# Transposes of probabilities, first-layer rows, gathered rows and returning rows as float32r in a fused attention, expert and feed-forward kernel

## The chip, the cores and the metric

One core of one Trainium2 chip runs the whole program. The metric is device time in microseconds (us) of one execution. Engine names are those of the profile: PE is the matrix engine, PEld its weight load, DVE the vector engine, ACT the scalar engine, POOL the GpSimd engine, SP the engine whose queue issues most transfers.

## What is computed

Attention over 2 batches of 8 heads (576 positions, head width 64, rotary positions on q and k), then a mixture of 8 experts of which each of the 1152 tokens takes one, then a feed-forward layer. All in float32:

```python
scores = scale * np.matmul(q_rot, k_rot.transpose(0, 1, 3, 2))
scores = scores - np.max(scores, axis=-1, keepdims=True)
attn = np.exp(scores)
attn = attn / (np.sum(attn, axis=-1, keepdims=True) + 1e-09)
x = np.matmul(attn, v)                       # to (1152, 512)
expert_idx = np.argmax(xn @ en.T / tau, axis=1)
...
h = np.maximum(x[mask] @ w1[e], 0.0)         # 512 -> 1024
out[mask] = gate_w[mask, None] * (h @ w2[e]) # 1024 -> 512
...
h = out @ w_in                               # 512 -> 2048
g = np.maximum(h, 0.0) + np.log1p(np.exp(-np.abs(h)))
y = g @ w_out
```

## The kernel before, in words

The order of instructions on every engine is the order in which the program is written; nothing reorders them. The precise products are made of float32r matmuls on operands that are split in two: a high part (ACT casts to float32r) and a low part (DVE subtracts the high part from the value).

**Attention** (to 187 us in the trace). The 16 heads run in 8 pairs. A pair has 9 steps, one for each block of 128 query rows (the fifth is shared by the two heads); with 72 steps in all, t = 0 to 71. In step t the program emits, in this order: the exponential of step t (`softmax_exp`, ACT L539, into a tile p of 128 x 576), the evictions left over from the step before (among them the p-tail: ACT L432 and DVE L433), four transposes of p(t-1) on PE (`transp`, L545, into PSUM tile tp), the scores of step t+2 (`mm_s`, L529, into PSUM tile sc, of which there are two), some filler work on PE, the row maximum of step t+1 (`softmax_max`, DVE L533), the low part of the transposed step t-2 (`ev_lo`, DVE L563) and the high part of step t-1 (`ev_hi`, ACT L552). The tiles tp are two, so the transposes of one step wait until `ev_lo` of two steps before has read its tile. The filler work holds the products with v (`pv`, L590 to L592), the transposes of the last 64 columns of p (`tail`, L574, and `tail_shared`, L578), the transposes that prepare q and k of the next pair (`prep_bank`, L444 from ks as float32r, L448 from qq and L446 from t as float32) and the output products (`xout`, L606). The rotation of the next pair's q and k runs on POOL.

The tiles p come from a pool of eight buffers, which are handed out in turn; before the first p the pool gives out four of them to the expert embeddings (`embt`), their squares (`esq`) and two normalised copies (`en2`). A generator `egen` advances by one part in each of the steps 2 to 5; each part is one DVE scaling of embt (L641), the first one after a reciprocal.

**Routing** (187 to 198 us) picks the experts and sorts tokens into blocks of 128.

**Experts** (198 to 368 us). There are 13 blocks. For a block the rows are gathered (tile xg), transposed by 4 PE transposes (`x_t`, through `four`, L954) and split (`x_ev`); 24 matmuls of 512 columns make the first layer (L975); ACT applies the relu into tile hr (L982); 8 transposes (`h_t`, L954, reading every second column of hr) and a split give the operand of the second layer, 24 matmuls (L1004); ACT multiplies by the gate (L1011, tile yo), and POOL scatters the rows to memory (L1014, tensor ys). The weights of each expert are fetched and split in 8 pieces a block (ACT L936, DVE L940). The tile gates is copied from PSUM once (DVE L1097), before the first `y_out`.

**Feed-forward** (368 to 577 us). Rows come back from memory into tiles yr, 4 transposes each (`y_t`, L877), 9 in all, of which 5 are made while the last expert blocks run. Then two passes of matmuls (L1306, L1353).

A transpose is a matmul in which the data is the loaded operand (PEld) and an identity is streamed; `idf` is the identity in float32, `idr` in float32r:

```python
def transp(t):
    p = tiles['p', t]
    tp = tiles['tp', t] = ps_t.tile([P, 4, P], F32, tag="t", name="tp")
    for x in range(4):
        T.transpose(tp[:, x], p[:, x * P:x * P + P], idf)
```

Of the kernel before, what the change touches and what calls it, by code (L numbers as in the profile page):

```python
# [95 lines left out]
def moe_kernel(ctx: ExitStack, tc: tile.TileContext, q, k, v, emb, tau, w1, w2, w_in, w_out, rope, tab, out):  # L96
# [58 lines left out]
    rev = tb("rev").rearrange("p (c e) -> p c e", c=5)  # L155

# [162 lines left out]
    with actx:  # L319
# [4 lines left out]
        pp = actx.enter_context(tc.tile_pool(name="pp", bufs=8))  # L324
# [210 lines left out]
        def softmax_exp(t):  # L535
            _, g, hs = where(t)
            i, c = hs[0]
            p = tiles['p', t] = pp.tile([P, S], F32, tag="p", name="p")
            A.activation(p.rearrange("p (n t) -> p n t", n=2), tiles.pop(('sc', t))[:, :, 0:288], AF.Exp, bias=tiles.pop(('nm', t)), accum_out=head(i)['rst'][:, c:c + 1])  # L539

        def transp(t):
            p = tiles['p', t]
            tp = tiles['tp', t] = ps_t.tile([P, 4, P], F32, tag="t", name="tp")
            for x in range(4):
                T.transpose(tp[:, x], p[:, x * P:x * P + P], idf)  # L545
# [23 lines left out]
        def tail(i):  # L569

            j, a = divmod(i, 2)
            d = ps_m.tile([LEFT, 4, P], F32, tag="m", name="tail")
            for c in range(4):
                T.transpose(d[:, c], tiles.pop(('p', 9 * j + 5 * a + c))[:, 512:576], idf)  # L574
            return lambda: prep_k(last(j)[:, a, 0:512], d.rearrange("p c t -> p (c t)"), True)

        def tail_shared(j, bank):
            T.transpose(bank[0:LEFT], tiles.pop(('p', 9 * j + 4))[:, 512:576], idf)  # L578
            return lambda: prep_k(last(j)[:, :, 512:576], bank[0:LEFT].rearrange("p (a t) -> p a t", a=2))
# [50 lines left out]
        embt = pp.tile([E, DM], F32, tag="p", name="embt")  # L630
# [3 lines left out]
        esq = pp.tile([E, DM], F32, tag="p", name="esq")  # L634
        en2 = [pp.tile([E, 4, 2, D], F32, tag="p", name="en2") for _ in range(2)]
# [85 lines left out]
        for t in range(NS + 5):  # L721
# [55 lines left out]
            if 1 <= t <= NS:  # L777
                ev_hi(t - 1)
            do_late()
# [35 lines left out]
            if 2 <= t <= 5:  # L815
                next(egen, None)
# [49 lines left out]
    def y_load(p, t, **cond):  # L866

        yr = yr3[t % 4]
        r = (TOK_PASSES[p][0] + t) * P
        return yr, SY.dma_start(yr, ys[r:r + P], **cond)  # L870

    def y_t(p, t, yr, pool, tag):
# [3 lines left out]
        for k in range(4):  # L876
            T.transpose(pt[:, k], yr[:, k * P:(k + 1) * P], idf)  # L877
# [15 lines left out]
    if True:  # L893
# [8 lines left out]
        xgs = [xg_.tile([P, DM], F32, name=f"xg{i}") for i in range(3)]  # L902
        for t in xgs:
            G.memset(t, 0.0)
# [43 lines left out]
        def gather(n):  # L948
            G.indirect_dma_start(xgs[n % 3][:, :], None, xs[:, :], bass.IndirectOffsetOnAxis(idx[:, n:n + 1], axis=0), bounds_check=NT - 1, oob_is_err=False)

        def four(src):
            pt = ps_x.tile([P, 4, P], F32, tag="x", name="pt")
            for k in range(4):
                T.transpose(pt[:, k], src(k), idf)  # L954
# [23 lines left out]
        def relu(n):  # L978
            ph = hs.pop(n)
            h = hs[n] = xe.tile([P, FF], F32, tag="hr", name="hr", bufs=1)  # L980
            for i in range(2):
                A.activation(h[:, 512 * i:512 * i + 512], ph[i], AF.Relu)  # L982

        def h_t(n):
            h = hs.pop(n)
            return [four(lambda k: h[:, 512 * i + 256 * (k // 2):512 * i + 256 * (k // 2) + 256].rearrange("p (q r) -> p q r", r=2)[:, :, k % 2]) for i in range(2)]
# [105 lines left out]
        def between(n):  # L1092
            if n == 1:
# [3 lines left out]
                V.tensor_copy(gates, pgat)  # L1097
                xctx.close()
                ypool = ctx.enter_context(tc.tile_pool(name="ypool", bufs=1, side="right", reuse_waits="tile"))
                yr3.extend(ypool.tile([P, DM + 1], F32, name=f"yr{i}") for i in range(4))  # L1100
                ypools.append(ypool)
                for t in yr3:
                    G.memset(t, 0.0)
# [125 lines left out]
        x_ev(3, x_t(3))  # L1229
# [215 lines left out]
```

## Time and profile before

| | us |
|---|---|
| median of three runs | 580.10 |
| the three runs | 579.31, 580.10, 581.25 |
| the profiled execution's own time | 579.42 |
| its span in the trace | 577.6 |
| PE busy | 545.6 (94%) |
| DVE busy | 454.3 (79%) |
| ACT busy | 438.6 (76%) |
| POOL busy | 199.9 (35%) |

The span runs from the first to the last record of the trace; 1.8 us of the execution's own time lie around it. Shares are means over stages that have different limits, so a stage's limit is read from the stretch itself. Matmuls overlap, so the time from one PE row's start to the next one's start says more than the duration printed. "xN" on a row counts N instructions of the same kind in a row; the bracket at a row's end is the idle time of that engine before it and what ended it.

### The profile page before, as it was taken

How to read it: one execution, taken by the hardware profiler on the slowest of the kernel's cores; microseconds unless marked ns; L12 is line 12 of the kernel's file. 1: busy time of each engine (PE TensorE's matmuls, PEld its weight loads, DVE VectorE, ACT ScalarE, POOL GpSimd, SP SyncE). 2: the span in 40 equal slices, each digit the busy share in tenths (PEclk: the TensorE clock that was granted, in tenths of full speed). 3: DMA queues.
4: the chain of work that ended last, by engine and by line, in shares of the span. 5: the costliest groups of instructions: out<-in, count | busy, mean ns of one | idle time of the engine just before them, and what ended most of it. 6: DMA issues, size and time to landing. Idle time of an engine off the chain costs nothing. (4 is left out here: it accounts for less than half of the span.)

```text
span 577.6 us, 9874 instructions
## 1 busy us (share of the span) xinstructions
PE 545.6 (94%) x3277; PEld 478.7 (83%) x3277; DVE 454.3 (79%) x757; ACT 438.6 (76%) x832; POOL 199.9 (35%) x304
## 2 busy tenths in 40 slices
PE   5789999999998799999999999999999999999995
PEld 4679999999987688887777888887889999888994
DVE  6988788787977779989999998778876766687243
ACT  2678878877775599789988998698877877677550
POOL 7999998749731330332222421300000000000033
PEclk8799999999999899999999999999999999999998
DMA  5414000061332545892439895263323222000012
GB/s 152 132 61 109 24 1 2 2 204 53 111 114 95 188 129 169 305 345 74 177 117 320 304 364 199 82 226 109 110 78 106 73 74 75 35 1 0 2 73 91
DMA packets 37269, 70.54 MB, mean 122 GB/s; under 512 B 8146, under 2 KB 23890, under 8 KB 37088
## 3 DMA queue, kind: packets, MB, share of 16 engines
q1 hardware_dynamic: 34272, 62.64, 32.5%
q0 software_dynamic: 2800, 7.09, 3.6%
q8 instruction: 26, 0.43, 0.3%
q10 hardware_dynamic: 144, 0.16, 0.2%
q14 instruction: 27, 0.22, 0.1%
HBM read 91.11 MB, written 8.13 MB: 172 GB/s over the span
## 5 line engine op out<-in xcount | busy, mean ns | idle before, releaser
L940 DVE TENSOR_TENSOR wt<-raw,wt 128x1024 fp32r<-128x1024 f32 x100 | 116.5, 1220 | 8.7 <-ACT wt L936 8.6
L1306 PE MATMUL ph<-yt,wt 128*128 128x320 f32 (+1 forms) x576 | 105.4, 336 | 2.2 <-ACT r__5778 L1318 1.4
L936 ACT CAST wt<-raw 128x1024 fp32r<-128x1024 f32 x100 | 98.7, 1066 | 6.6 <-DMA raw<-in_moe_w_dram 6.6
L1353 PE MATMUL po<-wt,g 128*128 128x512 f32 x432 | 103.6, 391 | 0.0
L1306 PEld LDWEIGHTS ph<-yt,wt 128*128 128x128 f32 x576 | 93.5, 188 | 11.6 <-ACT r__5778 L1318 1.8
L1353 PEld LDWEIGHTS po<-wt,g 128*128 128x128 f32 x432 | 80.3, 188 | 16.7 <-ACT g L1337 0.3
L1004 PE MATMUL py<-wt,ht 128*128 128x512 f32 x312 | 76.0, 396 | 2.6 <-DVE wt L940 2.6
L1370 POOL DMA_INDIRECT out_dram<-acc,otok x9 | 9.6, 1070 | 186.2 <-DVE acc L1367 185.6
L1004 PEld LDWEIGHTS py<-wt,ht 128*128 128x128 f32 x312 | 57.6, 188 | 15.4 <-DVE wt L940 3.9
L975 PE MATMUL ph<-wt,xt 128*128 128x512 f32 x288 | 69.3, 395 | 0.0
L539 ACT ACTIVATE p<-sc,nm 128x576 f32<-128x576 f32 x72 | 53.9, 749 | 14.4 <-DVE nm L533 13.8
L975 PEld LDWEIGHTS ph<-wt,xt 128*128 128x128 f32 x288 | 53.2, 188 | 10.8
L533 DVE TENSOR_REDUCE nm<-sc 128x1 f32<-128x576 f32 x72 | 54.2, 752 | 2.9 <-PE sc L529 1.7
L552 ACT CAST ph<-tp 128x512 fp32r<-128x512 f32 (+1 forms) x80 | 42.8, 547 | 14.9 <-PE tp L545 14.4
L529 PE MATMUL sc<-kt,qt 128*128 128x288 f32 x256 | 52.0, 327 | 1.6 <-ACT p L539 0.8
L545 PE MATMUL tp<-idf,p 128*128 128x128 f32 x288 | 45.1, 280 | 4.7 <-DVE pl L563 3.3
L563 DVE TENSOR_TENSOR pl<-tp,ph 128x512 fp32r<-128x512 f32 (+1 forms) x80 | 49.5, 627 | 0.1
L379 POOL TENSOR_TENSOR t<-qk,ropet 128x256 f32<-128x256 f32 x58 | 42.3, 757 | 10.9 <-DMA qk<-in_k_dram 10.4
L1337 ACT CAST g<-e 128x512 fp32r<-128x512 f32 (+2 forms) x33 | 21.7, 659 | 29.6 <-PE po L1353 20.2
L1338 DVE TENSOR_TENSOR g<-e,g 128x512 fp32r<-128x512 f32 (+2 forms) x33 | 24.3, 740 | 23.7 <-ACT g L1337 23.5
L529 PEld LDWEIGHTS sc<-kt,qt 128*128 128x128 f32 x256 | 38.1, 199 | 2.8 <-ACT p L539 1.3
L590 PE MATMUL po<-ph,vs 128*128 128x288 f32 x128 | 36.6, 307 | 3.8 <-DVE kt L433 1.4
(238 smaller groups left out, 1004.7 us busy)
## 6 DMA issues: line engine op xcount, KB each, us to landing
raw<-in_moe_w_dram SPq DMA_DIRECT2D x116, 512.0 KB
raw<-in_moe_w_in_dram SPq DMA_DIRECT2D x16, 512.0 KB
raw<-in_moe_w_out_dram SPq DMA_DIRECT2D x16, 512.0 KB
yr<-ys SPq DMA_DIRECT2D x9, 256.5 KB
qk<-in_k_dram SPq DMA_DIRECT2D x8, 256.0 KB
qk<-in_q_dram SPq DMA_DIRECT2D x8, 256.0 KB
vv<-in_v_dram SPq DMA_DIRECT2D x8, 256.0 KB
xs<-xrow SPq DMA_DIRECT2D x1, 1024.0 KB
```

The source lines that it names most:

```text
L529: T.matmul(sc[:, n, 0:288], lhsT=w, rhs=r, start=(x == 0), stop=(x == len(mm) - 1))
L533: V.tensor_reduce(nm, tiles['sc', t][:, :, 0:288], axis=AX.XY, op=ALU.max, negate=True)
L539: A.activation(p.rearrange("p (n t) -> p n t", n=2), tiles.pop(('sc', t))[:, :, 0:288], AF.Exp, bias=tiles.pop(('nm', t)), accum_out=head( ...
L545: T.transpose(tp[:, x], p[:, x * P:x * P + P], idf)
L552: A.copy(columns(head(i))['ph'][:, :, c * P:c * P + w], tp[:, :, x * w:x * w + w])
L563: V.tensor_tensor(hd['pl'][:, :, sl], tp[:, :, x * w:x * w + w], f(hd['ph'][:, :, sl]), op=ALU.subtract)
L936: A.copy(wt[:, 0], raw)
L940: (eng or V).tensor_tensor(wt[:, 1], raw, f(wt[:, 0]), op=ALU.subtract)
L975: T.matmul(ph[i], lhsT=xt[:, a, c], rhs=wt[:, r, 512 * i:512 * i + 512] if n else wt[r][:, 512 * i:512 * i + 512], start=(c == 0 and a == ...
L1004: T.matmul(py, lhsT=ht[c // 2][:, a, k], rhs=rhs[:, s], start=(c == 0 and r == 0 and a == 0 and s == 0), stop=(c == 3 and r == 1 and a == 1))
L1306: T.matmul(phs[i][:, 0:n1 - n0], lhsT=wt[:, a, k], rhs=yts[p][:, r, k, n0:n1], start=(k == 0 and a == 0 and r == 0), stop=(k == 3 and a == 1))
L1353: T.matmul(outs[i][c], lhsT=g[:, a, c * P:c * P + P], rhs=wt[:, r], start=(first and a == 0 and r == 0), stop=(last and a == 1))
```

## The change

Four kinds of transposes change type: those of p (`transp`), of hr (`h_t`), of xg (`x_t`) and of yr (`y_t`) stream the float32r identity and write float32r, over the same bits. The transposes of the last 64 columns of p stay in float32, as do those of qq and t.

To declare the same bytes as float32r, p gets a column more (577) and a second tile `pr` over the same buffer, and DVE sets the extra column to zero: one MEMSET of 128 x 1 for each step (72), placed behind `ev_lo` of that step. All transposes of p, tails included, are made to wait for that MEMSET. hr gets the same (one MEMSET for each block, in `relu`). xg and yr are declared float32r directly.

The pool of p has now eight named buffers instead of a turn. embt lies in p5, esq in p4, the two en2 in p6 and p7; steps 0 to 5 write p0 to p5, so the exponential of step 5 writes the buffer of embt. The generator egen advances once in steps 2 and 3 and twice in step 4.

One block is compared: the gathered rows of block 3 are transposed a second time in float32 (4 more PE transposes), ACT copies the result, DVE compares it with the float32r one and reduces to one number for each row, and a DVE instruction adds 1e30 times that to one column of gates.

```diff
-        pp = actx.enter_context(tc.tile_pool(name="pp", bufs=8))
+        pp = actx.enter_context(tc.tile_pool(name="pp", bufs=1))
+        slots = itertools.chain((f"p{i % 6}" for i in range(10)), itertools.cycle(f"p{i}" for i in (6, 7, 4, 5, 0, 1, 2, 3)))
...
-            p = tiles['p', t] = pp.tile([P, S], F32, tag="p", name="p")
+            slot = tiles['slot', t] = next(slots)
+            p = tiles['p', t] = pp.tile([P, S + 1], F32, tag=slot, name="p")[:, 0:S]
...
+        def rounded(t):
+
+            p = pp.tile([P, S + 1], F32R, tag=tiles.pop(('slot', t)), name="pr")
+            tiles['pad', t] = V.memset(f(p[:, S:]), 0.0).ins.name
+            tiles['p', t] = p
...
-                T.transpose(tp[:, x], p[:, x * P:x * P + P], idf)
+                after(T.transpose(tp[:, x].bitcast(F32R), p[:, x * P:x * P + P], idr), tiles['pad', t])
...
-                T.transpose(d[:, c], tiles.pop(('p', 9 * j + 5 * a + c))[:, 512:576], idf)
+                after(T.transpose(d[:, c], f(tiles.pop(('p', 9 * j + 5 * a + c))[:, 512:576]), idf), tiles.pop(('pad', 9 * j + 5 * a + c)))
...
-        embt = pp.tile([E, DM], F32, tag="p", name="embt")
+        embt = pp.tile([E, DM], F32, tag="p5", name="embt")
...
-        esq = pp.tile([E, DM], F32, tag="p", name="esq")
-        en2 = [pp.tile([E, 4, 2, D], F32, tag="p", name="en2") for _ in range(2)]
+        esq = pp.tile([E, DM], F32, tag="p4", name="esq")
+        en2 = [pp.tile([E, 4, 2, D], F32, tag=f"p{6 + x}", name="en2") for x in range(2)]
...
+            if t < NS:
+                rounded(t)
             do_late()
...
-            if 2 <= t <= 5:
+            for _ in range((0, 0, 1, 1, 2)[t] if t < 5 else 0):
                 next(egen, None)
...
-            T.transpose(pt[:, k], yr[:, k * P:(k + 1) * P], idf)
+            T.transpose(pt[:, k].bitcast(F32R), yr[:, k * P:(k + 1) * P], idr)
...
-        def four(src):
+        def four(src, pad=None):
             pt = ps_x.tile([P, 4, P], F32, tag="x", name="pt")
             for k in range(4):
-                T.transpose(pt[:, k], src(k), idf)
+                after(T.transpose(pt[:, k].bitcast(F32R), src(k), idr), pad)
...
+            h = xe.tile([P, FF + 1], F32R, tag="hr", name="hrr", bufs=1)
+            hs[n] = h, V.memset(f(h[:, FF:]), 0.0).ins.name
...
                 V.tensor_copy(gates, pgat)
+                V.scalar_tensor_tensor(gates[:, 3:4], differs, 1e30, gates[:, 3:4], op0=ALU.mult, op1=ALU.add)
...
-        x_ev(3, x_t(3))
+        px = x_t(3)
+        pt2 = ps_x.tile([P, 4, P], F32, tag="x", name="pt2")
+        for k in range(4):
+            T.transpose(pt2[:, k], f(xgs[0])[:, k * P:(k + 1) * P], idf)
+        x_ev(3, px)
+        other = gate_tmp()
+        differs = w([P, 1], "differs")
+        A.copy(other, pt2.rearrange("p a b -> p (a b)"))
+        V.tensor_tensor(other, px.rearrange("p a b -> p (a b)"), other, op=ALU.not_equal)
+        V.tensor_reduce(differs, other, axis=AX.X, op=ALU.max)
```

In `gather`, the load of yr and the two clearings on POOL only the declared type changes.

What moves on the engines, as the two programs have it. First DVE in steps 4 and 5 of attention (kt, vs: the next pair's k and v; nm: a row maximum; pl: low part; p with a number and tail: the p-tail; en: the scaled embeddings). Before:

```order
L533 TENSOR_REDUCE nm<-sc 128x1
L563 TENSOR_TENSOR pl<-tp,ph 128x4x128
L433 TENSOR_TENSOR kt<-own,kt 64x2x64
L392 TENSOR_TENSOR vs<-vv,vs 128x4x64
L641 TENSOR_SCALAR en_180<-embt,est 8x4x64
L433 TENSOR_TENSOR p_454<-tail,p_454 64x512
```

After:

```order
L539 TENSOR_REDUCE nm<-sc 128x1
L576 TENSOR_TENSOR pl<-tp,ph 128x4x128
L551 MEMSET pr 128x1
L439 TENSOR_TENSOR kt<-own,kt 64x2x64
L398 TENSOR_TENSOR vs<-vv,vs 128x4x64
L654 TENSOR_SCALAR en_180<-embt,est 8x4x64 x2
L439 TENSOR_TENSOR p_465<-tail,p_465 64x512
```

The fourth scaling of the embeddings stands directly behind the third and ahead of the p-tail, and a MEMSET stands behind `ev_lo`.

Second, DVE in the expert stage around the copy of gates (ht, xt: low parts of the transposed rows; wt: low part of a weight piece). Before:

```order
L959 TENSOR_TENSOR ht<-pt,ht 128x512 x2
L940 TENSOR_TENSOR wt<-raw_2864,wt 128x1024
L1097 COPY gates<-bank 128x16
L940 TENSOR_TENSOR wt<-raw_2865,wt 128x1024
L940 TENSOR_TENSOR wt<-raw_2866,wt 128x1024
L940 TENSOR_TENSOR wt<-raw_2867,wt 128x1024
L959 TENSOR_TENSOR xt<-pt,xt 128x512
```

After:

```order
L974 TENSOR_TENSOR ht<-pt,ht 128x512 x2
L955 TENSOR_TENSOR wt<-raw_3008,wt 128x1024
L1114 COPY gates<-bank 128x16
L1115 SCALAR_TENSOR_TENSOR gates<-differs,gates 128x1
L955 TENSOR_TENSOR wt<-raw_3009,wt 128x1024
L955 TENSOR_TENSOR wt<-raw_3010,wt 128x1024
L955 TENSOR_TENSOR wt<-raw_3011,wt 128x1024
L999 MEMSET hrr 128x1
L974 TENSOR_TENSOR xt<-pt,xt 128x512
```

An instruction on gates is added behind the copy, and the block's MEMSET ahead of xt. The two instructions of the comparison stand some rows earlier, behind the low part of block 3's rows:

```order
L974 TENSOR_TENSOR xt<-pt,xt 128x512
L1255 TENSOR_TENSOR junk<-pt,junk 128x512
L1256 TENSOR_REDUCE differs<-junk 128x1
L955 TENSOR_TENSOR wt<-raw_3004,wt 128x1024
L955 TENSOR_TENSOR wt<-raw_3005,wt 128x1024
```

There the program before goes from xt to the four pieces of wt directly.

## Rows read from the trace of the kernel before

**Rows 1.** Busy time by stretch: engines with counts, granted PE clock, DMA share, GB/s.
```profile
16.00:31.50 15.50, 10.25 (x61) 8.56 (x60) 14.65 (x27) 10.73 (x27) 15.06 (x24) 0.85 0.35 91
73.06:93.23 20.17, 19.75 (x160) 18.80 (x160) 16.38 (x32) 16.50 (x42) 19.06 (x33) 1.00 0.01 2
255.00:312.00 57.00, 54.39 (x264) 44.74 (x263) 56.10 (x64) 52.43 (x72) 15.64 (x15) 1.00 0.48 168
```

**Rows 2.** Groups of the page: busy us, mean ns, then idle before and releaser.
```profile
L533 DVE TENSOR_REDUCE nm<-sc 128x1 f32<-128x576 f32 x72 | 54.2, 752 | 2.9 <-PE sc L529 1.7
...
L545 PE MATMUL tp<-idf,p 128*128 128x128 f32 x288 | 45.1, 280 | 4.7 <-DVE pl L563 3.3
```

**Rows 3.** Timeline of PE: start, duration, instruction; a step with three float32 blocks.
```profile
60.02 0.77 PE L529 MATMUL sc<-kt,qt 128*128 128x288 f32 x4
...
61.06 0.60 PE L448 MATMUL pt<-idf,qq 128*128 128x128 f32 x4
...
61.86 0.38 PE L529 MATMUL sc<-kt,qt 128*128 128x288 f32 x1
```

**Rows 4.** Timeline of PE: the same step with one block as float32r.
```profile
48.66 0.77 PE L529 MATMUL sc<-kt,qt 128*128 128x288 f32 x4
...
49.62 0.54 PE L444 MATMUL pt<-idr,ks 128*128 128x128 f32 x4
...
50.38 0.38 PE L529 MATMUL sc<-kt,qt 128*128 128x288 f32 x1
```

**Rows 5.** Timeline of one pair, 73.06 to 93.23: first row, waits, last row.
```profile
73.06 0.66 PE L545 MATMUL tp<-idf,p 128*128 128x128 f32 x4
...
83.02 0.40 PE L590 MATMUL po<-ph,vs 128*128 128x288 f32 x1 [0.22 <-DVE p L433]
...
93.22 0.31 PEld L545 LDWEIGHTS tp<-idf,p 128*128 128x128 f32 x3 [0.35 <-DVE pl L563]
```

**Rows 6.** Timeline around the exponential of step 5 (26.74).
```profile
26.74 0.74 ACT L539 ACTIVATE p<-sc,nm 128x576 f32<-128x576 f32 x1 [0.44 <-PE tail L574]
...
27.47 0.57 ACT L432 CAST p<-tail 64x512 fp32r<-64x512 f32 x1
...
27.82 0.88 DVE L641 TENSOR_SCALAR en<-embt,est 8x256 f32<-8x256 f32 x1
...
28.73 0.69 DVE L433 TENSOR_TENSOR p<-tail,p 64x512 fp32r<-64x512 f32 x1
...
31.57 0.40 PE L590 MATMUL po<-ph,vs 128*128 128x288 f32 x1 [1.45 <-DVE kt L433]
...
31.76 0.41 DVE L641 TENSOR_SCALAR en<-embt,est 8x256 f32<-8x256 f32 x1
```

**Rows 7.** Busy time by stretches of 2 us there, with the granted clock.
```profile
23.00:25.00 2.00, 0.61 (x3) 0.64 (x4) 2.00 (x6) 0.98 (x3) 2.00 (x3) 0.77 0.01 3
25.00:27.00 2.00, 2.00 (x11) 1.70 (x9) 1.97 (x4) 1.04 (x3) 1.92 (x5) 0.50 0.59 146
27.00:29.00 2.00, 1.93 (x14) 1.44 (x12) 1.94 (x4) 2.00 (x6) 2.00 (x3) 0.88 0.13 30
29.00:31.00 2.00, 0.66 (x4) 0.42 (x4) 1.94 (x4) 1.12 (x4) 2.00 (x4) 1.00 0.00 0
```

**Rows 8.** Timeline: a DVE MEMSET of 128 x 1 at the start.
```profile
2.94 0.06 DVE L133 MEMSET half<- 128x1 f32 x1
```

**Rows 9.** Timeline of ACT: the first and third gate multiplication of the experts.
```profile
236.80 0.69 ACT L1011 ACTIVATE yo<-py,gates 128x512 f32<-128x512 f32 x1 [3.72 <-DVE gates L1097]
...
253.42 0.69 ACT L1011 ACTIVATE yo<-py,gates 128x512 f32<-128x512 f32 x1 [1.67 <-DMA ys<-yo,dest]
```

**Rows 10.** Timeline of PE late in the experts.
```profile
304.21 5.56 PE L1004 MATMUL py<-wt,ht 128*128 128x512 f32 x23 [0.56 <-DVE wt L940]
```

**Rows 11.** Weight loads of transposes by tile: duration ns min/median/max, first and last start.
```profile
L954 PEld LDWEIGHTS pt<-idf,hr x104: 194/209/209, 207.2 to 358.4; 128*128 128x128 f32 x104
...
L444 PEld LDWEIGHTS pt<-idr,ks x48: 138/140/142, 49.6 to 159.7; 128*128 128x128 f32 x48
```

## What I expect of the change, and why

> **What bounds the kernel now.** I read busy time by stretch first. In one pair of heads from the steady part of attention PE is busy 19.75 of 20.17 us while DVE and ACT are busy some 16.4 [rows 1]: PE sets the pace there. The first stretch, 16.0 to 31.5, is another case: DVE is busy 14.65 of 15.50 and PE only 10.25 [rows 1]. In the experts DVE is full, 56.10 of 57.00 us from 255 to 312 [rows 1], until PE starts to run back to back at 304.21 [rows 10]. So the change meets three limits: what it saves on PE counts in attention and late in the experts, what it adds on DVE counts at the start and in the experts up to 304.
>
> Then I asked which of the 72 transpose blocks of p (288 transposes [rows 2]) lie on the path. In the pair from 73.06 to 93.23 I followed the waits: PE runs through until it waits 0.22 for the p-tail of DVE at 83.02, and at 93.22 its weight load waits 0.35 for a low part [rows 5]; beside these two PE has no wait of 0.2 or more there. Two stretches of the pair, ahead of 83.02 and ahead of 93.22, therefore run through ACT and DVE (a block, its exponential and p-tail, the DVE tail), and three of nine blocks stand in them. Six of nine are on PE's path. From 31.57 on, 7 pairs and a bit are of this kind: I count 45 blocks.
>
> **What a block saves.** The trace has the swap itself. A step of four score matmuls and three transpose blocks, two of them in front of the same neighbours, takes 61.86 − 60.02 = 1.84 us with L448 as float32 [rows 3], and 50.38 − 48.66 = 1.72 us where L444 as float32r stands in its place [rows 4]. So 0.12 us for each block of four. Seven steps of the first kind take 1.84 to 1.85, six of the second 1.71 to 1.73. The bounds: from the start of the swapped block to the end of the step it is 61.86 − 61.06 = 0.80 [rows 3] against 50.38 − 49.62 = 0.76 [rows 4], which would be 0.04; the upper end is 0.14, the step's figure and the 0.02 by which such steps differ. I take 0.12, the whole step, because the start of a row inside a step is partly modelled, and the steps follow one another without a wait.
>
> Beside this the skill has a rule against the change. The Trainium skill, "TensorE: Matmul & The Clock Gate", section "LDWEIGHTS (loading the stationary operand)", gives a weight load as its columns divided by 1.2 in ns, whatever the type; that makes an estimate of 107 ns for 128 columns, just the float32 pace, and the saving would be nothing. The trace does not agree: 0.80 us for two blocks is 0.10 for a transpose [rows 3], and the step with one of them as float32r is 0.12 shorter [rows 4]. That nothing is saved is a rival below.
>
> **The sum, against the profiled execution's own 579.42** (0.7 under the median):
>
> 1. Attention: 45 blocks × 0.12 = 5.4. POOL is busy 19.06 of the pair's 20.17 [rows 1], so a pair can't shrink by more than about 1.1 before POOL is late; 6 × 0.12 = 0.72 fits, but not everywhere. I take nine tenths: **−4.9** (−1.6 at 0.04 a block, −6.3 at 0.14 and all 45).
>
> 2. The MEMSETs. A DVE MEMSET of this shape takes 0.06 [rows 8]. Each stands behind a low part and waits for the exponential of its own step, which by the timeline had ended before the instruction behind that low part began in every step, so the wait costs nothing. The 72 lie mostly under DVE's idle time, 3.8 us a pair [rows 1]. They count where PE's next block waits for that low part anyway (93.22 [rows 5]) or where DVE is full at the start: once a pair and in five early steps. **+0.4** (0.2 to 4.3, if all counted).
>
> 3. The start. The exponential of step 5 starts at 26.74 [rows 6]. After the change it writes the buffer of embt, so it waits for the last scaling of embt. That one has moved up from 31.76 to directly behind the third (27.82 plus 0.88; the one at 31.76 takes 0.41 [rows 6]). So the exponential can't start before about 29.2, 2.4 later. Behind it on ACT wait its p-tail (27.47 [rows 6]), behind that DVE's p-tail, 28.73 + about 2.0, and then the chain of DVE's next row maximum, low part and k, and PE's products at 31.57, which wait for it [rows 6]. What is not on that chain: the scaling itself is done at 31.76 before, so DVE has 0.4 less to do later. I take **+2.0** (1.3 to 2.4).
>
> 4. The clock. In the stretch 23 to 25 PE is busy 0.61 of 2.00 and the granted clock falls from the higher level (2.4 GHz) to 0.50, the lower (1.2 GHz), and stays there to 27 and beyond [rows 7]. Counted from the shares of the windows, (1 − 0.77) × 2 / 0.5 + 2.00 + (1 − 0.88) × 2 / 0.5 = 3.4 us at the lower level. PE's next idle stretch, 29 to 31, is busy 0.66 and the clock stays up [rows 7]. With term 3 it is 2 us longer, from about 29 (27 to 29 is still busy 1.93 [rows 7]) to 33.6 with one block in it, and I think the clock falls again. 3.4 us of PE's pace at half speed give 1.7 less work: **+1.7** (0 if it stays up, 3.4 for a stretch of twice the length).
>
> 5. Experts. The comparison puts two instructions of 128 x 512 on DVE. Their bounds are the subtraction of a 64 x 512 tile, 0.69 [rows 6], and the row maximum at 0.752 × 512/576 = 0.67 [rows 2], and the instruction on gates, 128 x 1, costs between the MEMSET's 0.06 [rows 8] and 0.2. Together some 1.5, a little of it overlapped: +1.3. DVE is what the first gate multiplication waits for (3.72 for gates [rows 9]), its rows are scattered, the third one waits for that scatter's landing (1.67 at 253.42 [rows 9]), and from there DVE is full: nothing gives it back. Bounds 0.6 (if half is given back at the waits for gates) and 1.6. The MEMSETs of the 5 blocks up to 304 add 0.06 each: +0.3. The four float32 transposes, 0.40 [rows 3], and ACT's copy, some 0.57 as its p-tail [rows 6], lie beside DVE, which is the later one there, and cost nothing; on the path they would be 1.0. From 304.21 PE is back to back: three gathered and five returning blocks, 8 × 0.12 = −0.96, and −0.1 for the early ones. For hr I take nothing: its loads take 209 ns in place of 140 [rows 11], since they read every second column, and that pace may hold; the bound is that of two blocks of four, 0.24 for eight, five times, −1.2. Sum: **+0.5** (−1.4 to +1.2).
>
> 6. Feed-forward and routing: the four later returning blocks stand under ACT's evictions and transfers: 0.
>
> −4.9 + 0.4 + 2.0 + 1.7 + 0.5 = −0.3, so 579.1 for an execution like the profiled one, and 0.7 more for the median: **579.8**.
>
> **The rivals.** *The clock stays up* (no term 4). For it: the stretch 29 to 31 shows low activity with no fall [rows 7]. Against it: the stretch grows. 579.8 − 1.7 = 578.1, faster.
>
> *Half is saved*, 0.06 a block. This is the case that ends slower: the new wait of the exponential for embt at 26.74 and the comparison cost 2.0 + 1.3, the clock 1.7, and with 0.06 a block attention gives back 2.4 and the experts 0.5. 579.8 + 2.5 + 0.5 = 582.8. It turns slower by more than 0.3% below some 0.08 a block (2.0 lost on 45 × 0.9 and 8 blocks). For it: the bound of 0.04 from the block's own start [rows 3, 4]; against it: the whole step, and the blocks of tp stand in other company than the one that was swapped.
>
> *The change doesn't do what it says*: the weight load sets the pace and float32r saves nothing. Terms 1 and the late part of 5 vanish: 579.8 + 4.9 + 1.1 = 585.8. Against it are rows 3 and 4. This is the skill's rule above.
>
> *More is saved*: hr's loads get faster with the type as well (−1.2), the start loses 1.3 in place of 2.0, and the clock stays up: 579.8 − 1.2 − 0.7 − 1.7 = 576.2.
>
> **How the numbers follow.** Forecast 0.40, clock stays up 0.27, half saved 0.16, more saved 0.12, nothing saved 0.05. About 0.3% (1.7 us) is what a measurement of this kernel can tell from no change: under 578.4 is faster, over 581.8 slower. Faster: half of the case at 578.1 (0.14), all of 576.2 (0.12), a tenth of the forecast (0.04): 0.30. Slower: most of the half saved (0.13), nothing saved (0.05), a little of the forecast with a longer fall of the clock (0.04): 0.22. Same: 0.48. The range goes from 576.0 to 582.8, which leaves out the case of nothing saved and half of the one of more saved. The forecast's own range is 578.4 to 581.5.
>
> **What would show it.** In the profile after: steps with three blocks of 1.60 to 1.72 in place of 1.84 (term 1); the exponential of step 5 near 29.2 with DVE's en as its releaser (3); granted clock of 0.5 in a stretch around 31 to 36 (4); the pair near 19.5 (1 and 2); the first gate multiplication relative to routing 1.3 later (5). The prediction is wrong if the pair doesn't shrink (POOL or the DVE tails then hold it), if the start loses nothing, or if the step of three blocks stays at 1.84.

## The result: 583.1 us, 0.6% slower

The changed kernel takes 583.11 us in the median of nine runs (582.41 to 588.10), the kernel before 580.10 (nine runs, 578.85 to 581.25). The ratio is 1.0064, 95% interval 1.0038 to 1.0090: slower and clear of the noise of these runs, and 0.3 us outside the range of the forecast. The profiled execution of the changed kernel took 584.52 with a span of 582.7, so its span is 5.1 longer than that of before where the medians differ by 3.0; it is one of the longer ones of its kind, and the places below are to be read for where time went, the medians for how much.

Where it went, by the same instruction in both traces (start in us; the lag is after less before; the last column is the lag less that of the row above, so it is what a stretch added; expert blocks are counted from 0):

| instruction | before | after | lag | added in the stretch |
|---|---|---|---|---|
| row maximum of step 3 | 19.23 | 17.75 | −1.48 | −1.5 |
| row maximum of step 6 | 29.45 | 30.91 | +1.46 | +2.9 |
| row maximum of step 13 | 45.83 | 50.84 | +5.01 | +3.6 |
| row maximum of step 71 | 177.31 | 180.73 | +3.42 | −1.6 |
| first layer of block 1 | 204.65 | 207.94 | +3.29 | −0.1 |
| first layer of block 3 | 230.26 | 234.62 | +4.36 | +1.1 |
| first layer of block 9 | 310.93 | 315.62 | +4.69 | +0.3 |
| feed-forward, back to back | 393.45 | 398.48 | +5.03 | +0.3 |

Three things stand out: the start loses 5.0, all of attention behind it gives back only 1.6, and the late experts, which were to give back about 1, lose 0.3. The 1.5 us by which step 3 is early are no gain of the change: the changed kernel is 0.9 ahead at step 0 already (11.26 against 12.12), and over all profiled runs that start varies from 0.9 early to 0.2 late.

**The start.** Timeline of the changed kernel around the exponential of step 5 (its lines are 7 to 13 higher than before):

```profile
27.16 1.67 DVE L654 TENSOR_SCALAR en<-embt,est 8x256 f32<-8x256 f32 x2
...
28.86 0.74 ACT L546 ACTIVATE p<-sc,nm 128x576 f32<-128x576 f32 x1 [4.72 <-DVE en L654]
...
30.19 0.68 DVE L439 TENSOR_TENSOR p<-tail,p 64x512 fp32r<-64x512 f32 x1 [1.36 <-ACT p L438]
...
33.05 0.61 PE L603 MATMUL po<-ph,vs 128*128 128x288 f32 x1 [1.01 <-DVE kt L439]
```

The exponential is released by the second of the two scalings, at 28.86 where it stood at 26.74 [rows 6]: the wait that the sum had foreseen. What comes behind it was not foreseen in size. The granted clock by stretches of 2 us (PE, PEld, DVE, ACT, POOL busy with counts, clock, DMA share, GB/s):

```profile
18.00:20.00 2.00, 0.74 (x7) 0.77 (x7) 2.00 (x7) 1.02 (x3) 1.88 (x4) 1.00 0.59 172
20.00:22.00 2.00, 0.53 (x4) 0.24 (x3) 1.88 (x6) 0.77 (x3) 1.84 (x4) 0.94 0.83 256
22.00:24.00 2.00, 1.40 (x8) 1.43 (x8) 2.00 (x5) 1.55 (x5) 2.00 (x3) 0.50 0.12 26
...
34.00:36.00 2.00, 2.00 (x12) 1.93 (x11) 1.00 (x4) 0.17 (x1) 1.92 (x3) 0.50 0.64 206
...
40.00:42.00 2.00, 2.00 (x10) 2.00 (x9) 1.36 (x3) 0.33 (x2) 1.92 (x4) 0.50 0.00 0
42.00:44.00 2.00, 2.00 (x19) 1.97 (x18) 0.94 (x2) 1.55 (x5) 1.84 (x4) 0.94 0.67 166
```

The same from 8 to 46, the kernel before and then the changed one:

```profile
8.00:46.00 38.00, 30.04 (x197) 26.44 (x198) 33.76 (x64) 24.87 (x63) 36.55 (x57) 0.87 0.40 114
```

```profile
8.00:46.00 38.00, 27.40 (x160) 23.92 (x160) 30.87 (x67) 20.20 (x54) 36.55 (x58) 0.73 0.41 112
```

The clock goes to its lower level at the end of the stretch 20 to 22 and stays there to 42, some 20 us in a row; in the kernel before it was low for 3.4 there [rows 7] and for some 7 earlier. While PE has little to do (to 32) that costs little. From 34 on PE is busy all the time, so the 8 us up to 42 at half speed are worth an estimated 4; the table has 3.6 from step 6 to step 13.

**Attention.** The page has the transposes at 258 ns each where they had 280 [rows 2], and their wait has moved from the low part to the MEMSET behind it:

```profile
L558 PE MATMUL tp<-idr,pr 128*128 128x128 f32 x288 | 38.3, 258 | 5.0 <-DVE pr L551 3.6
```

One pair takes 19.86 in place of 20.17 [rows 1]: 0.31 less, not 0.72.

```profile
80.09:99.95 19.86, 19.44 (x161) 18.36 (x161) 16.42 (x42) 16.45 (x41) 16.69 (x27) 1.00 0.01 2
```

The step with three blocks shows what a block really saves:

```profile
84.65 0.77 PE L535 MATMUL sc<-kt,qt 128*128 128x288 f32 x4
85.26 0.60 PE L587 MATMUL tail<-idf,pr 128*64 128x128 f32 x4
85.69 0.60 PE L454 MATMUL pt<-idf,qq 128*128 128x128 f32 x4
86.05 0.54 PE L558 MATMUL tp<-idr,pr 128*128 128x128 f32 x4
86.42 0.76 PE L535 MATMUL sc<-kt,qt 128*128 128x288 f32 x4
```

86.42 − 84.65 = 1.77 against 1.84 [rows 3]: 0.07 to 0.08. That is the best of the steps. From the first score matmul of one step to that of the next (from 75.51 in the kernel before, from 80.09 in the changed one) the nine steps of the pair save 0.07, 0.05, 0.08, 0.00, 0.02, 0.05, −0.02, 0.02 and 0.04. Three of them (the fourth, seventh and eighth) lie ahead of the two places where the prediction saw PE wait; they give 0.00 together, and the other six 0.31, or 0.05 each: its count of six in nine held, its price did not. The weight loads say why it isn't 0.12. First the changed kernel, then the swap of the kernel before on which the price was built (PEld: start, duration, four loads a row):

```profile
85.58 0.47 PEld L454 LDWEIGHTS pt<-idf,qq 128*128 128x128 f32 x4
86.02 0.42 PEld L558 LDWEIGHTS tp<-idr,pr 128*128 128x128 f32 x4
```

```profile
49.14 0.46 PEld L574 LDWEIGHTS tail<-idf,p 128*64 128x64 f32 x4
49.60 0.42 PEld L444 LDWEIGHTS pt<-idr,ks 128*128 128x128 f32 x4
49.96 0.42 PEld L545 LDWEIGHTS tp<-idf,p 128*128 128x128 f32 x4
50.35 0.43 PEld L529 LDWEIGHTS sc<-kt,qt 128*128 128x128 f32 x3
```

A float32 block is 86.02 − 85.58 = 0.44 from its first load to the next block's. The float32r block in the swap is 49.96 − 49.60 = 0.36, which is 0.08 less, and the float32 block **behind** it is 50.35 − 49.96 = 0.39, which is 0.05 less. The swapped step thus held two gains: that of the block, and that of a float32 block that follows a float32r one. In the changed kernel the blocks of p are float32r themselves, so a step that had such a follower loses the second gain: the step of [rows 4] takes 1.72 there, and 93.30 to 95.03, 1.73, in the changed kernel, as its last block had already been cheap.

**The experts.** Weight loads late in the experts: a returning block, the eight transposes of hr, the first layer. First the kernel before, then the changed one:

```profile
322.21 0.58 PEld L877 LDWEIGHTS pt<-idf,yr 128*128 128x128 f32 x4
322.76 1.03 PEld L954 LDWEIGHTS pt<-idf,hr 128*128 128x128 f32 x8
323.70 0.20 PEld L975 LDWEIGHTS ph<-wt,xt 128*128 128x128 f32 x1
```

```profile
326.83 0.54 PEld L892 LDWEIGHTS pt<-idr,yr 128*128 128x128 f32 x4
327.31 1.19 PEld L969 LDWEIGHTS pt<-idr,hrr 128*128 128x128 f32 x8
328.45 0.30 PEld L990 LDWEIGHTS ph<-wt,xt 128*128 128x128 f32 x2
```

From its first load to the next block's, the returning block takes 327.31 − 326.83 = 0.48 in place of 0.55; the gathered blocks save the same 0.07. The eight transposes of hr take 328.45 − 327.31 = 1.14 in place of 323.70 − 322.76 = 0.94: float32r is **slower** here, by 0.19 to 0.20 a block. (The starts of PE's rows would make it 1.13 against 0.87, but with 0.29 against 0.44 for the returning block in front: part of the time only changes sides.) A whole late block, first layer to first layer, takes 328.48 − 315.62 = 12.86 where it had taken 323.74 − 310.93 = 12.81.

The comparison's four float32 transposes, which the sum had beside DVE and at nothing, stand on PE between two blocks that it works off back to back:

```profile
227.32 0.46 PE L969 MATMUL pt<-idr,xg 128*128 128x128 f32 x4
227.62 0.62 PE L1250 MATMUL pt<-idf,xg 128*128 128x128 f32 x4
228.00 5.77 PE L1021 MATMUL py<-wt,ht 128*128 128x512 f32 x24
```

228.00 − 227.62 = 0.38 us, part of the 1.1 that the table has from block 1 to block 3. Of the rest, 0.6 come from block 1 to block 2, where the kernel with hr in float32 (below) adds nothing.

### The profile page after: what moved, and what is told of

Read it like the earlier page. It is cut to its first block, busy times and chain, and to the rows that moved or that the text cites. A ratio compares the mean times of both kernels' runs of the same rounds, so it can differ in the third digit from the quotient of the medians.

```text
span 582.7 us, 9984 instructions
## 1 busy us (share of the span) xinstructions
PE 548.2 (94%) x3281; PEld 479.3 (82%) x3281; DVE 457.5 (79%) x845; ACT 438.9 (75%) x833; POOL 198.3 (34%) x304
## 5 line engine op out<-in xcount | busy, mean ns | idle before, releaser
L558 PE MATMUL tp<-idr,pr 128*128 128x128 f32 x288 | 38.3, 258 | 5.0 <-DVE pr L551 3.6
L603 PE MATMUL po<-ph,vs 128*128 128x288 f32 x128 | 37.9, 317 | 3.5 <-DVE p L439 1.4
```

## The experiments

The theory from the two traces: the wait of the exponential costs 2 us and lengthens the clock's fall; a block saves 0.05 to 0.08; the strided blocks of hr lose 0.25 each; the comparison costs 1.2. Rivals: the clock falls because shorter transposes leave PE less busy, or by chance; the MEMSETs eat the gain; DVE hides the rest. Ratios are to runs of the kernel before on the same chip, with 95% intervals. The kernel before took 579.84, 580.12 and 580.51 us on the three chips of the experiments, so a difference in us between two of them can be off by up to 0.7 for that alone.

### The wait taken out, and the wait alone

```diff
 # the changed kernel: embt's buffer first needed in step 9
-        slots = itertools.chain((f"p{i % 6}" for i in range(10)), itertools.cycle(f"p{i}" for i in (6, 7, 4, 5, 0, 1, 2, 3)))
+        slots = itertools.chain((f"p{i}" for i in range(5)), itertools.cycle(f"p{i}" for i in (0, 1, 2, 3, 5, 6, 7, 4)))
...
-            for _ in range((0, 0, 1, 1, 2)[t] if t < 5 else 0):
+            if 2 <= t <= 5:
```

> The changed kernel, but the embeddings keep a buffer that no exponential needs before step 9, and their four scalings stand in steps 2 to 5 as in the kernel before. Theory (the wait of step 5's exponential for the embeddings costs 2 us and leaves PE idle long enough that the clock stays at its lower level for some 20 us in place of 10): the exponential of step 5 near 26.7, lower level some 10 us in all, about 579 us. Rival A (the long low stretch comes from PE being less busy with shorter transposes): the stretch stays near 20 us and only the 2 us of the wait go, about 581. Rival B (the start differs between executions by chance): no change, 583.

Measured 581.59 (12 runs, 578.75 to 583.96), 1.0018 (0.9992 to 1.0044). The exponential starts at 26.62 again, released by PE's tail. The row maximum of step 13 starts at 48.41, still 2.6 late, and the clock over the start is at

```profile
8.00:46.00 38.00, 28.90 (x177) 25.77 (x178) 33.63 (x70) 22.73 (x57) 36.55 (x57) 0.78 0.40 113
```

where the changed kernel has 0.73 there and the kernel before 0.87. So the wait is a part, and something else keeps the clock low: by the time it is rival A that comes nearest, and the theory's 579 is missed.

The other half is the kernel before with that sharing and the early scaling alone, all transposes float32:

```diff
 # the kernel before; the pool and its other tiles get the names that they have in the change
-            p = tiles['p', t] = pp.tile([P, S], F32, tag="p", name="p")
+            p = tiles['p', t] = pp.tile([P, S], F32, tag=next(slots), name="p")
...
-        embt = pp.tile([E, DM], F32, tag="p", name="embt")
+        embt = pp.tile([E, DM], F32, tag="p5", name="embt")
...
-            if 2 <= t <= 5:
+            for _ in range((0, 0, 1, 1, 2)[t] if t < 5 else 0):
```

> The kernel before with one thing of the change alone: the named buffers with the embeddings in the one of step 5, and the fourth scaling in step 4. All transposes float32, no MEMSETs, no comparison. Theory: exponential of step 5 some 2 us late and the clock low for much longer than before, 583 to 586 us. Rival A: the 2 us of the wait alone, 582. Rival B: as before, 580.

Measured 583.94 (6 runs), 1.0072 (1.0045 to 1.0099). Its exponential of step 5:

```profile
29.59 0.74 ACT L541 ACTIVATE p<-sc,nm 128x576 f32<-128x576 f32 x1 [3.15 <-DVE en L643]
```

The row maximum of step 6 is 2.2 late (31.63), that of step 13 4.1 (49.90), and nothing more is added over the rest of attention (181.28 against 177.31). Two us are the wait, two the clock that falls behind it: the windows have it at its lower level from 31.2 to 38, 6.8 us, where it stays up in the kernel before. This one edit, which has nothing to do with transposes, is worth 4.1 us, more than the whole loss of the change.

### float32r in attention against the MEMSETs

```diff
-after(T.transpose(tp[:, x].bitcast(F32R), p[:, x * P:x * P + P], idr), tiles['pad', t])
+after(T.transpose(tp[:, x], f(p[:, x * P:x * P + P]), idf), tiles['pad', t])
```

> The changed kernel with the 72 blocks of p transposed as float32, their MEMSETs and waits kept. Theory (0.08 us saved for a block on the path, MEMSETs dear by at most 0.1 a pair): a pair takes 20.2 to 20.3 us against 19.85 in the changed kernel and 20.17 before, so 585.5 to 586. Rival (the float32r saving is the full 0.12 for six blocks, and the waits for the MEMSETs eat half of it): a pair takes 20.5 or more, 588. Rival B (the blocks are hidden): 583.

Measured 586.20 (5 runs), 1.0114 (1.0090 to 1.0138): float32r in attention is worth 3.1 us to the changed kernel (2.9 by the ratios). With the MEMSETs but float32 a pair takes

```profile
53.50:73.70 20.20, 19.79 (x162) 18.78 (x161) 16.46 (x40) 16.45 (x42) 19.04 (x32) 1.00 0.06 18
```

and from step 13 to step 71 it is 131.56 (180.83 − 49.27) against 131.48 in the kernel before. The 58 MEMSETs of that stretch cost 0.1 in all. They eat nothing, and with 3.1 us gained the blocks aren't hidden either: both rivals fall. Of the 3.1 the two traces place only 1.7, between steps 13 and 71 (131.56 against 129.89), and the start takes 1.6 of that back (step 13 at 49.27 here, at 50.84 in the changed kernel). In these two executions (585.88 and 584.52) what is left, 1.4, lies in the experts, where one trace can't settle it: between the first layers of blocks 5 and 6 this one loses 1.6 on the kernel before, those of three other kernels 1.0 to 1.3, and the remaining eight between −0.6 and 0.5. No edit goes with it, and why stays open.

### What else lowers the clock

With the wait gone the start is still late by 2.6. The wait and float32r in attention were undone together:

```diff
 # the changed kernel with the slots and scalings of the first run, and
-after(T.transpose(tp[:, x].bitcast(F32R), p[:, x * P:x * P + P], idr), tiles['pad', t])
+after(T.transpose(tp[:, x], f(p[:, x * P:x * P + P]), idf), tiles['pad', t])
```

> The changed kernel with the embeddings in a buffer that is not waited for and the blocks of p in float32, MEMSETs kept: against the first run it undoes float32r in attention alone, against the run with p in float32 the wait alone. Theory (shorter transposes leave PE less busy in the first 30 us and the clock low for longer): mean granted clock back near 0.986, no delay at 45 us, and the time 586.2 less 4, about 582 us. Rival (MEMSETs or the order of DVE lower the clock): mean clock 0.979 as in the first run, 2 us late at 45 us, 584 us.

Measured 582.85 (12 runs), 1.0044 (1.0025 to 1.0063). The clock at the start and the place of step 13 are those of the kernel before:

```profile
8.00:46.00 38.00, 30.17 (x196) 26.45 (x197) 34.34 (x77) 24.93 (x63) 36.55 (x58) 0.87 0.39 112
```

The row maximum of step 13 starts at 45.88 (45.83 before). The mean granted clock of whole executions says the same of all runs, not of one trace: median 0.985 here, 0.985 to 0.987 for the kernel before, 0.979 with float32r and no wait, 0.978 and 0.980 with the wait and float32 (the kernel with the wait alone and the one with p in float32), 0.975 in the changed kernel. So the second cause is float32r itself, in the first 30 us, where DVE sets the pace [rows 1] and PE's shorter blocks save nothing. The traces show how it acts. The clock falls near 24 in the kernel before, here, and in the run with float32r and no wait. With float32 blocks it is back by 28, with float32r ones only past 30. From 24 to 32 it is at 0.79 in the first two and at 0.60 in the third. The time, 582.85, lies between theory and rival. In this trace, level with the kernel before at step 71 (0.1), routing adds 1.1 and the experts 1.7. By the ratios float32r is still worth 1.5 us without the wait (1.0018 against 1.0044), but those intervals overlap: what it costs at the start is known in size from single traces and from the second kernel below.

Two kernels put that to the test. They start from one in which three parts are set right (below, 578.1 us). The first makes each block of p in steps 0 to 7 three times over, in the same place:

```diff
-            for x in range(4):
+            for x in range(4 * (3 if t < 8 else 1)):
+                x %= 4
```

> The kernel of the run before this one, with the transposes of p in the first eight steps made three times (the same bits written to the same place), 64 more PE instructions where PE is idle. Theory (the clock falls there because PE is idle in parts of the first 30 us): fewer or shorter stretches at the lower level up to 45 us, 1 to 3 us less than that kernel. Rival (the clock's fall does not depend on it): the same stretches, and the time 0 to 2 us longer for the added work.

Measured 577.86 (12 runs, 576.33 to 581.18), 0.9960 (0.9942 to 0.9979). The mean clock rises from 0.9775 to 0.983; the time hardly moves (0.3 us). From 24 to 32, the kernel that it starts from and then this one:

```profile
24.00:32.00 8.00, 6.33 (x29) 5.24 (x30) 7.80 (x18) 5.77 (x15) 7.92 (x13) 0.57 0.18 44
```

```profile
24.00:32.00 8.00, 6.50 (x46) 5.97 (x47) 7.79 (x19) 5.68 (x15) 7.92 (x13) 0.79 0.16 44
```

The clock is back where float32 has it, and so is the row maximum of step 7: 32.22, against 33.71 in the kernel that it starts from and 32.10 in the kernel before. Then the added work takes the gain back: three tripled blocks stand where PE is busy without a pause (2.00 in every stretch of 2 us from 32 to 42), the first from 33.02 to 34.08, 1.06 where a single one takes 0.37 (33.12 to 33.49), and by step 10 the kernel is 1.9 late. More work on PE, in the same place and with the same bits, thus shortens the low stretch. The second leaves the blocks of steps 0 to 7 in float32:

```diff
+                if t < 8:
+                    after(T.transpose(tp[:, x], f(p[:, x * P:x * P + P]), idf), tiles['pad', t])
+                else:
                     after(T.transpose(tp[:, x].bitcast(F32R), p[:, x * P:x * P + P], idr), tiles['pad', t])
```

> The same kernel (578.1 us) with the blocks of p as float32 in the first eight steps and float32r behind them. Theory (PE busier in the first 30 us keeps the clock up): mean clock 0.983 to 0.987, delay at 45 us under 1 in place of 1.9, 577 us. Rival: clock and time as without it, 578.1 us.

Measured 575.81 (6 runs, 574.44 to 577.99), 0.9935 (0.9909 to 0.9960): the fastest of all, 0.65% under the kernel before.

```profile
8.00:46.00 38.00, 30.42 (x201) 26.60 (x201) 34.57 (x76) 25.37 (x65) 36.55 (x57) 0.87 0.41 112
```

Clock 0.87 at the start, mean 0.987, and the row maximum of step 13 at 45.45, 0.4 ahead of the kernel before. The clock from 24 to 32 is 0.79, and the row maximum of step 7 starts at 31.74. The slower instruction, in eight steps of 72, makes the program 2.3 us faster (1.9 by the ratios, whose intervals overlap a little; 3.2 against the kernel with the comparison put back, below, on the same chip).

### The transposes of hr

```diff
+        def four32(src):
+            pt = ps_x.tile([P, 4, P], F32, tag="x", name="pt")
+            for k in range(4):
+                T.transpose(pt[:, k], src(k), idf)
+            return pt
...
-            h = xe.tile([P, FF + 1], F32R, tag="hr", name="hrr", bufs=1)
-            hs[n] = h, V.memset(f(h[:, FF:]), 0.0).ins.name
 # and h_t calls four32 in place of four
```

> The changed kernel with the transposes of hr as float32 again and without hr's MEMSET. Theory (a float32r transpose that reads every second column is paced by its load at 0.14 us, a float32 one at 0.12): the block of eight 0.88 us in place of 1.13, five late blocks give 1.2 back, 581.9 us. Rival (weights on DVE set the pace there): blocks shorter but the same time, 583.

Measured 582.72 (7 runs), 1.0051 (1.0027 to 1.0076): 0.4 less than the changed kernel by the medians, which the intervals don't separate. In its trace the lag falls from 4.92 at block 9 to 4.36 in the feed-forward, where that of the changed kernel rises from 4.69 to 5.03: 0.9 of the 1.2 that the theory asked for. The theory's step was too large: it came from the starts of PE's rows. From load to load the eight float32 transposes take 0.94 here too (327.51 to 328.45), 0.19 less than in the changed kernel, and five times that is 0.9. The next edit is the stronger one: the relu writes even and odd columns apart, so the transposes read neighbours.

```diff
-A.activation(h[:, 512 * i:512 * i + 512], ph[i], AF.Relu)
+A.activation(h[:, 512 * i:512 * i + 512].rearrange("p (g r q) -> p g r q", g=2, r=2), ph[i].rearrange("p (g q r) -> p g r q", g=2, r=2), AF.Relu)
...
-            return [four(lambda k: h[:, 512 * i + 256 * (k // 2):512 * i + 256 * (k // 2) + 256].rearrange("p (q r) -> p q r", r=2)[:, :, k % 2], pad) for i in range(2)]
+            return [four(lambda k: h[:, 512 * i + 128 * k:512 * i + 128 * k + 128], pad) for i in range(2)]
```

> The changed kernel, but the relu writes the rows of hr with their even and odd columns apart, so that the eight float32r transposes read 128 neighbouring columns each. Theory (the reading of every second column sets the pace of 0.14 us, a load of neighbouring columns 0.085): a block of eight takes 0.70 us in place of 1.13, five late blocks give 2.1 us back, 581.0 us. Rival (the pace comes from float32r behind float32r matmuls, whatever the columns): block and time unchanged.

Measured 581.66 (12 runs), 1.0025 (1.0003 to 1.0046): 1.5 less than the changed kernel by the medians. Its trace at the same place:

```profile
336.68 0.46 PE L892 MATMUL pt<-idr,yr 128*128 128x128 f32 x4
336.97 0.85 PE L969 MATMUL pt<-idr,hrr 128*128 128x128 f32 x8
337.65 1.60 PE L990 MATMUL ph<-wt,xt 128*128 128x512 f32 x6
```

337.65 − 336.97 = 0.68 for eight, and a whole late block, first layer to first layer, takes 12.39 (325.26 to 337.65) in place of 12.86. Loads by tile, the changed kernel and then this one:

```profile
L969 PEld LDWEIGHTS pt<-idr,hrr x104: 194/195/202, 210.5 to 363.4; 128*128 128x128 f32 x104
```

```profile
L969 PEld LDWEIGHTS pt<-idr,hrr x104: 138/140/144, 208.2 to 358.9; 128*128 128x128 f32 x104
```

So the columns decide: 0.14 a transpose when every second one is read, 0.085 when neighbours are, both float32r. The rival (the pace comes from what stands ahead) falls.

### The comparison

```diff
-V.scalar_tensor_tensor(gates[:, 3:4], differs, 1e30, gates[:, 3:4], op0=ALU.mult, op1=ALU.add)
...
-    T.transpose(pt2[:, k], f(xgs[0])[:, k * P:(k + 1) * P], idf)
...
-A.copy(other, pt2.rearrange("p a b -> p (a b)"))
-V.tensor_tensor(other, px.rearrange("p a b -> p (a b)"), other, op=ALU.not_equal)
-V.tensor_reduce(differs, other, axis=AX.X, op=ALU.max)
```

> The changed kernel without the comparison of one block and without the instruction on gates that uses it. Theory (its 1.2 us on DVE lie on the path of the first scatter and are not given back): 1.1 to 1.3 us less, 581.9 us; the expert stage begins to lag behind the kernel before by 1.1 less from 230 us on. Rival (DVE has slack there, the waits take it back): 583.

Measured 583.28 (8 runs), 1.0062 (1.0037 to 1.0087): no gain. In the changed kernel the two instructions stand on DVE as costed:

```profile
231.64 0.68 DVE L1255 TENSOR_TENSOR junk<-pt,junk 128x512 f32<-128x512 f32 x1
232.35 0.69 DVE L1256 TENSOR_REDUCE differs<-junk 128x1 f32<-128x512 f32 x1
232.96 4.62 DVE L955 TENSOR_TENSOR wt<-raw,wt 128x1024 fp32r<-128x1024 f32 x4
...
241.43 0.16 DVE L1115 SCALAR_TENSOR_TENSOR gates<-differs,gates 128x1 f32<-128x1 f32 x1
```

Without them the first gate multiplication starts at 239.50 in place of 241.43, but the second one has a new wait:

```profile
239.50 0.69 ACT L1028 ACTIVATE yo<-py,gates 128x512 f32<-128x512 f32 x1 [3.09 <-DVE gates L1114]
249.62 0.69 ACT L1028 ACTIVATE yo<-py,gates 128x512 f32<-128x512 f32 x1 [2.29 <-DMA ys<-yo,dest]
```

It waits 2.29 for the first scatter to land, and at 249.62 it is later than with the comparison (249.38). This trace was 0.6 ahead before the comparison's place (block 1 at 207.33 against 207.94), so of the 1.9 at the first gate multiplication 1.3 are the comparison's, as the sum had them. At the third one (257.15 against 257.98) 0.2 are left: here the wait for the transfer takes most of the gain. The other way round, the same lines were put into the kernel that was set right (its diff is this one with + for −):

> The kernel with three parts set right (578.1 us), with the comparison of one block put back. Theory (its DVE time is not given back): 1.1 to 1.3 us more, 579.3 us. Rival (the run without the comparison showed no gain against the changed kernel because DVE's delay is taken back at the wait for the scatter): 578.1 us.

Measured 578.99 (12 runs), 0.9976 (0.9951 to 1.0000), against 578.14 without it: 0.85 more (0.5 by the ratios), with intervals that overlap. By the medians of both pairs the comparison costs between 0 and 1 us. The traces of this pair say more: from block 1 to the feed-forward the kernel with the comparison gains 0.5 on the kernel before and the one without it 2.0, a difference of 1.5, of which 0.7 falls on that place between blocks 5 and 6. What the comparison costs, and whether a wait gives it back, stays open.

### Three parts set right

No wait for embt, no comparison, hr's columns apart, that is the diffs of the first run, of the run without the comparison and of hr's columns together:

> The changed kernel with three parts set right: the embeddings in a buffer that is not waited for, no comparison, and hr's columns apart. Theory: the clock and the wait give back 1.5 to 4, the comparison 1.2, hr's blocks 2.1: 576 to 578 us, faster than the kernel before by the 2.3 us of attention and about 1 us of the experts. Rival (the clock falls more often as PE is less busy, and takes what the transposes save): 580.

Measured 578.14 (12 runs, 574.85 to 581.40), 0.9968 (0.9946 to 0.9989): faster than the kernel before by 2.0 us, 5.0 faster than the changed kernel, and just over what was expected; the clock is still low for longer at the start (0.82 over 8 to 46 us, mean 0.9775).

## Why the prediction was wrong, point by point

The forecast was 579.8, no change that can be measured, and is 3.3 us too low; the rival "half is saved" named 582.8. Its price of 0.06 a block was about right, but that it comes within 0.3 of the result is partly luck: it has too little for the clock and for hr, and more for the comparison than the runs can show.

1. **Attention's saving: the step that failed.** "So 0.12 us for each block of four" and "I take 0.12, the whole step". On PE's path a block saves 0.02 to 0.08, 0.05 in the mean, a pair 0.31, and from step 13 to step 71 the kernel saves 1.6 us where the term had 4.9 for little more. This is the largest miss of the sum. The count of six blocks in nine was right. The reading of the step was right too; it held a gain of 0.05 that belonged to the float32 block behind the swapped one, and that the change does away with by making the followers float32r. The lower bound of 0.04 that the text had beside it, from the block's own start to the end of the step, was the better reading in some steps.

2. **MEMSETs**: +0.4 was forecast (by the text's own count, once a pair and five early steps at 0.06, it would be 0.7), 0.1 measured from step 13 to step 71. That their wait costs nothing was right.

3. **The start**: +2.0 forecast, 2.1 to 2.2 by the kernel with the wait alone. Right, in place and size.

4. **The clock**: a fall behind the longer idle stretch was forecast, for 3.4 us and a cost of 1.7. With the wait alone it came for 6.8 us and a cost of 1.9: the mechanism and nearly the cost. In the profiled execution of the changed kernel it was some 20 us and 3.6. The cost in the six profiles with the wait was between 1.0 and 3.6 from step 6 to step 13, and there is a second cause that the prediction did not name: the shorter transposes themselves, in a stretch where DVE sets the pace. The prediction counted blocks in that stretch as worth nothing; they are worth less than nothing. Without the wait, the three profiles with single float32r blocks there are 1.7 to 2.6 late at step 13, the two with float32 blocks −0.4 and 0.05.

5. **Experts**: +0.5 forecast, 1.7 measured (3.29 to 5.03 of lag). The returning and the gathered blocks save 0.07 each where the sum had 0.12, so 0.6 in place of 0.96 for the eight late ones. For hr "I take nothing", with a bound of −1.2 on the good side only; it is +0.19 a block, 0.9 in the five late ones, and 0.6 early (from block 1 to block 2). The row of 209 ns had shown that reading every second column costs more, and nothing excluded a loss. The comparison, +1.3 in the sum, is worth 0 to 1 by the medians and up to 1.5 by the traces; its four transposes on PE, put at nothing, take 0.38 on PE's path.

6. Feed-forward and routing: nothing in the sum, and 0 measured for the feed-forward. Between step 71 and block 1 the traces differ by 1 us either way, from one execution to another.

The loads do set the pace of these transposes: with the relu's columns apart, only the reading of the loaded operand changed on PE, and the pace went from 0.14 to 0.085. The Trainium skill, "TensorE: Matmul & The Clock Gate", section "LDWEIGHTS (loading the stationary operand)", gives the time of a load by its columns, without a word on the type, an estimate of 107 ns for 128. The traces agree for float32 with neighbouring columns, 0.44 / 4 = 0.11 a load (the prediction's 0.10 came from the starts of PE's rows), and differ elsewhere: 0.085 for float32r, and with every second column 0.12 for float32 (0.94 for eight) and 0.14 for float32r.

## What to carry to other kernels

A price taken from one swapped instruction group holds for its neighbours as they were; look at the rows of the next group as well, and ask whether the change alters that one too. A shorter instruction on an engine that is not the bound can lose time: here shorter transposes kept the matrix engine's clock low for longer in a stretch that DVE bounds. Use the faster form where the engine sets the pace, and leave the slower one where it waits. And what a change brings along to make room (a shared buffer, an instruction moved ahead) is to be costed like the change itself; here it cost 4.1 us, more than float32r in attention brought (3.1).

## What the runs showed that was not expected

- float32r transposes that read every second column are slower than float32 ones: 1.14 against 0.94 for eight from load to load, and 0.68 with neighbouring columns.
- A float32 block behind a float32r one is 0.05 shorter (0.39 against 0.44 from load to load).
- Eight steps of float32 transposes at the start in place of float32r ones, 32 transposes, take the mean clock from 0.9775 to 0.987 and some 2 us off the time.
